# Two attentions on one core: first loads in halves, later weight rounding, and a third memory query moved into the attention turns

## The chip, the cores and the metric

The kernel runs on one core of a Trainium2 chip. The metric is device time in microseconds (us), the median of several executions. Profiles are of one execution; their times count from the start of the profiled span.

## The reference

Two independent attentions over 2048 tokens, 576 features, 32 heads of 18 features, all in float32. Their outputs stand side by side.

```
A:  q = x wq (32 heads);  k, v = x wk, x wv (one head for all)
    out = softmax(q k / sqrt(18)) v  wo
B:  q, k, v = x wq, x wk, x wv (32 heads each); 4 segments of 512 tokens; M = z = 0
    for s in 0..3:
        a_dot = causal softmax(q_s k_s / sqrt(18)) v_s
        a_mem = (phi(q_s) M) / (phi(q_s) z + 1e-6)        phi(t) = t + 1 if t > 0 else exp(t)
        o_s   = g a_mem + (1 - g) a_dot                   g = sigmoid(beta), one per head
        M, z += phi(k_s)^T v_s, sum of phi(k_s)
    out = o wo
```

Segment 0 has an empty memory. The memory queries of segments 1, 2 and 3 are the products `phi(q_s) M` (called num below) and `phi(q_s) z` (den).

## The kernel before, in words

**Stage 1, projections (0 to about 277 us of the span).** TensorE projects A's four chunks of 512 tokens (c = 0..3), then B's four segments (s = 0..3). A projection of 126 features is 14 matmuls, because operands are split in two rounded parts, high and low (`proj`, L261). For that, every input and weight is rounded by a copy (ScalarE or VectorE) and the rest is taken by a subtraction (VectorE or GpSimd).

- *First loads.* For c = 0 five pieces (k = 0..4, 128 rows each, the last 64) of A's weights `a_w` and of `a_xT` are loaded before anything can be multiplied. The weights and inputs go out on the SP queue, but the first input piece on ScalarE's queue.
- *B's weights* come in 15 pieces (`WPARTS`), loaded on GpSimd's queue (`load_wpart`) and rounded by `split_wpart`: a ScalarE copy (L251) and a GpSimd subtraction (L252). Pieces 10 to 14 are the query weights of the heads 0 to 27. They are rounded in segment 0, one behind each of the five key projections t = 0..4, and pieces 12 to 14 are loaded behind the first three. `pin` keeps an engine's pinned instructions in the order of the code, so a pinned copy that waits for its load holds up the pinned work behind it. Seven small loads of `gt` on GpSimd's queue follow.
- *A segment* is: five key projections (the fifth holds four query heads too), value projections of the first half of the heads, `last_key` and `fifth_bound` (small), second half of the values, four query projections. Every query projection is evacuated from PSUM (`pj`, four banks) by Relu, Abs, Exp and a rounding copy on ScalarE and three operations on VectorE.
- *The last segment* (s = 3) is written out on its own, pinned on TensorE. Between its query projections it asks the memory: `ask` multiplies phi(q) by M (one float32 matmul of 512 columns into `mm`, L444), `answer` scales the result on ScalarE (`nm`) and stores it; `total` multiplies by z (L592). `bound` (L588) multiplies magnitudes for the upper bound of the scores and needs the Abs of all five pieces. Only then come the first scores. The second half of the last segment's values is left to the attention stage (`late_value`, spread over its first 19 turns by `LATER`).

**Stage 2, attention (about 277 to 1350 us).** PE, ScalarE and VectorE follow an order written out by hand, in 416 turns of up to three score tiles. A block is four heads of a chunk of A (11 turns) or of a segment of B (2 turns). A0's turns are 0 to 10; B's blocks take turns 11 to 18, 30 to 37, 49 to 52, 64 to 71, 83 to 86 and so on. Per turn TensorE does the scores (L945 for A, L953 for B) into `E` (three tiles of two PSUM banks), at most one side job into the one bank `F`, and the products of the turn before the last into `O` (L993). ScalarE takes the exponentials (L963); one of three tiles is copied to SBUF by VectorE first (`W`, L960). In A-blocks two or three half tiles have their exponential computed on VectorE instead (`BY_DVE`, L919 to L926).

- *Side jobs.* From turn `ASK` = 20 on, `ask_memory` does the memory queries of the segments in `LATE_ASK` = (1, 2). Each segment has 6 steps of two halves; a turn takes a half: 4 column groups of 32 x 256 columns in float32 (L852). After the second half VectorE takes `F` out (L857, L861). Before the change a turn with B-scores takes no such half, so 24 halves occupy turns 20-29, 38-48 and 53-55. The queries' phi(q) come from DRAM (`qfB`, loaded by `load_qf` into a buffer `xh`, of which there are two, shared with the heads to be projected, `parts`).
- Then `out_proj` units fill the turns (L796, 8 instructions each, one unit per turn; 6 x 60 units), as soon as all five pieces of a chunk's heads are weighed by GpSimd (L780). What must happen at which turn is kept in a list `later`; `due` takes up to two entries a turn, and entries with a cost (the weighing) only when none of the next three turns is a B-turn and VectorE has no exponential open.

**The end.** Left-over units, then the output projections of A's last two chunks (L1280).

```
elif k >= ASK and all(its[n][0] == "A" for n, pr in turns[k]) and next(memory, None) is None:
    memory = None
```

## Time and profile before

| | before |
| --- | --- |
| median of 3 runs | 1394.51 us (1393.42 to 1395.25) |
| the profiled execution | 1394.57 us; its span 1392.9 us |
| granted TensorE clock | 0.999 |
| busy: TensorE / ScalarE / VectorE / GpSimd | 99% / 87% / 74% / 19% of the span |
| first matmul of a projection | 6.43 us |
| first scores (turn 0) | 276.80 us |
| first out_proj unit (turn 64) | 444.28 us |
| start of the last turn (415) | 1349.93 us |

A line of the timeline or of the chain begins with start and duration in us, then engine, line of the kernel, operation, what is written <- what is read. In brackets stands the idle time before it and what ended it. In the table of windows each engine has its busy us and, in brackets, its number of instructions.

### The profile page before, as it was taken

What the parts mean: (1) busy time and instruction counts of PE and PEld (TensorE: products, weight loads), DVE (VectorE), ACT (ScalarE), POOL (GpSimd) and SP (SyncE); (2) the same over time, 40 slices, a digit from 0 to 9 for tenths busy, and PEclk for the clock granted to TensorE, in tenths of its full rate; (3) what the DMA queues carried; (4) which work ended last, traced back from release to release, by engine and by line L of the source; (5) the groups of instructions that cost most, each with busy time, mean ns of one, the idle gap of its engine ahead of it and who ended that gap; (6) DMA issues with size and microseconds to landing.
All of it is one profiled execution on the core that took longest, in us unless ns stands there. A gap on an engine that the chain in (4) does not pass through costs nothing.

```text
span 1392.9 us, 41210 instructions
## 1 busy us (share of the span) xinstructions
PE 1379.1 (99%) x17455; PEld 835.6 (60%) x17455; DVE 1032.6 (74%) x1509; ACT 1205.8 (87%) x1497; POOL 260.5 (19%) x388
## 2 busy tenths in 40 slices
PE   9999999999999999999999999999999999999998
PEld 6778888755554555555555555555555555555558
DVE  6565463388787887777888877876878778887884
ACT  4543453599999999999999999999999999999992
POOL 2462120012313211312110022113010220001002
PEclk9999999999999999999999999999999999999999
DMA  9876556575564545332322442232103321120023
GB/s 285 261 230 185 180 198 204 188 208 181 153 182 158 147 145 162 101 113 77 105 67 71 141 152 63 85 120 79 52 35 100 104 76 42 31 71 21 18 64 132
DMA packets 88638, 173.67 MB, mean 125 GB/s; under 512 B 12308, under 2 KB 20109, under 8 KB 88018
## 3 DMA queue, kind: packets, MB, share of 16 engines
q1 hardware_dynamic: 81614, 158.91, 36.6%
q0 software_dynamic: 2368, 7.13, 1.8%
q10 hardware_dynamic: 4464, 4.92, 1.1%
q8 instruction: 139, 2.28, 0.7%
q14 instruction: 53, 0.43, 0.1%
HBM read 99.65 MB, written 70.67 MB: 122 GB/s over the span
## 4 chain that ended last, share of the span: by engine, by line
PE 88%; DVE 4%; ACT 3%; DMA 2%; issue 1%; POOL 1%; SPq 0%; DVEq 0%; POOLq 0%; ACTq 0%
PE O L993 33%; PE E L945 20%; PE F L796 11%; PE pj L261 11%; PE E L953 3%; ACT P L963 3%; PE nd L513 2%; DVE W L960 2%; PE pj L513 2%; PE E L1280 2%; PE pj L293 1%; PE F L852 1%; PE F L513 1%; DMA wr<-b_w 1%; DMA vseg<-vB 0%
## 5 line engine op out<-in xcount | busy, mean ns | idle before, releaser
L963 ACT ACTIVATE P<-E 128x1024 f32<-128x1024 f32 (+1 forms) x800 | 783.4, 1066 | 2.0 <-PE E L945 1.6
L960 DVE COPY W<-E 128x1024 f32<-128x1024 f32 (+2 forms) x416 | 453.1, 1089 | 142.2 <-PE E L945 84.1
L993 PE MATMUL O<-P,VA 128*32 128x256 f32 x7504 | 506.8, 379 | 0.0
L963 ACT ACTIVATE P<-W 128x1024 f32<-128x1024 f32 (+1 forms) x330 | 366.8, 1112 | 6.8 <-DVE W L960 6.3
L993 PEld LDWEIGHTS O<-P,VA 128*32 128x32 f32 x7504 | 258.8, 110 | 137.7 <-issue 4.7
L945 PE MATMUL E<-xl,kstA 56*128 56x512 f32 x1920 | 317.3, 430 | 2.1 <-ACT P L963 1.8
L945 PEld LDWEIGHTS E<-xl,kstA 56*128 56x128 f32 x1920 | 155.0, 184 | 159.1 <-issue 94.7
L968 POOL TENSOR_SCALAR_AFFINE_SELECT P<-P 128x256 f32<-128x256 f32 (+1 forms) x192 | 94.6, 493 | 393.4 <-ACT P L963 384.1
L780 POOL TENSOR_TENSOR xh<-xh,rb 126x512 f32<-126x512 f32 (+1 forms) x55 | 70.7, 1308 | 428.7 <-DVE PD L926 185.1
L796 PE MATMUL F<-woB,xh 126*32 126x192 f32 (+1 forms) x1920 | 126.6, 338 | 0.0
L993 PE MATMUL O<-PD,VA 128*32 128x256 f32 x688 | 88.9, 379 | 0.0
L796 PEld LDWEIGHTS F<-woB,xh 126*32 126x32 f32 (+1 forms) x1920 | 38.6, 108 | 74.8 <-issue 69.6
L993 PE MATMUL O<-P,vseg 128*32 128x256 f32 (+2 forms) x1536 | 81.4, 344 | 0.3
L127 DVE TENSOR_TENSOR qp<-pj,qp 126x512 fp32r<-126x512 f32 (+1 forms) x54 | 36.9, 686 | 54.4 <-ACT ph_e L408 32.8
L1002 DVE COPY oe<-O 128x512 f32<-128x512 f32 x64 | 44.2, 691 | 42.6 <-PE O L993 40.8
L261 PE MATMUL pj<-xh,wBh 128*126 128x512 f32 x180 | 72.5, 403 | 0.0
L919 DVE TENSOR_SCALAR PD<-E 128x512 uint32<-128x512 f32 x86 | 59.2, 688 | 16.5 <-PE E L945 14.9
L261 PE MATMUL pj<-xh,wBl 128*126 128x512 f32 x180 | 71.0, 394 | 0.0
L125 ACT CAST qp<-pj 126x512 fp32r<-126x512 f32 (+1 forms) x54 | 31.5, 584 | 42.6 <-PE pj L261 32.6
L993 PEld LDWEIGHTS O<-P,vseg 128*32 128x32 f32 x1536 | 49.1, 110 | 25.3 <-issue 1.8
L796 PE MATMUL F<-woA,xh 126*32 126x192 f32 (+1 forms) x960 | 63.9, 338 | 0.0
L924 DVE SCALAR_TENSOR_TENSOR PD<-PD,n 128x512 f32<-128x512 f32 x86 | 59.5, 692 | 3.0
(238 smaller groups left out, 1570.1 us busy)
## 6 DMA issues: line engine op xcount, KB each, us to landing
stB<-kB SPq DMA_DIRECT2D x96, 144.0 KB
stB<-qB SPq DMA_DIRECT2D x32, 288.0 KB
xl<-qA SPq DMA_DIRECT2D x30, 288.0 KB
oA<-oe SPq DMA_DIRECT2D x32, 256.0 KB
oB<-oe SPq DMA_DIRECT2D x32, 256.0 KB
qA<-qp SPq DMA_DIRECT2D x16, 504.0 KB
kB<-qp SPq DMA_DIRECT2D x16, 504.0 KB
qB<-qp SPq DMA_DIRECT2D x16, 504.0 KB
```

What stands on the lines that cost most here:

```text
L261: hold(nc.tensor.matmul(dst, w[:, c0 : c0 + M], x, start=i == 0, stop=i == len(ops) - 1))
L513: nc.tensor.matmul(pj[:, :n], x, w, start=m == 0, stop=m == len(ops) - 1)
L780: ins = tc.keep_in_program_order(nc.gpsimd.tensor_tensor(dst, a, b, op=op))
L796: nc.tensor.matmul(dst[32 * j : 32 * j + 32], parts[ab, c][: RT[t], t, r0 : r0 + 32], wo[ab][: RT[t], t, c0 : c0 + n], start=start, stop=stop,
L919: v.tensor_scalar(y, e, EXP_A, EXP_B, op0=ALU.mult, op1=ALU.add)
L924: lambda: stt(p, p, POLY[1], u, op0=ALU.add, op1=ALU.mult),
L945: nc.tensor.matmul(e[:, j], kstA[rows, 128 * kt : 128 * kt + 128], st[rows, h, :], start=True, stop=True)
L960: gate.append(nc.vector.tensor_copy(src[:, hs, :n], e[:, hs, :n]))
L963: nc.scalar.activation(p[:, hs, :n], src[:, hs, :n], AF.Exp, scale=SCALE)
L968: nc.gpsimd.affine_select(diag, diag, pattern=[[0, 2], [0, m], [1, 128]], base=0, channel_multiplier=-1, compare_op=ALU.is_ge, fill=0.0)
L993: nc.tensor.matmul(o[32 * j : 32 * j + 32, q0 : q0 + n], v, p[:, j % 2, p0 : p0 + n], start=m == hf == 0, stop=last and hf == 1,)
L1002: nc.vector.tensor_copy(osb, o)
```

## The change

- *First loads:* the first piece (k = 0) of inputs and weights is loaded in two halves of 64 rows, one half on SP's queue, one on ScalarE's, the inputs first. The other pieces stay on SP's queue.
- *B's query weights:* pieces 10 and 11 are rounded behind the key projections t = 1 and t = 3 of segment 0, pieces 12, 13 and 14 ahead of the value projections i = 1, 2, 3. The loads of 12 and 13 follow 10 and 11, the load of 14 follows 12.
- *Last segment:* `ask`, `answer`, `total` and the den store are gone. Its phi(q) are stored to `qfB[3]`, and `LATE_ASK` becomes (1, 2, 3). The condition that a turn be all A is dropped, so 36 halves occupy turns 20 to 55 without a gap. `load_qf(3)` comes at turn 32 or later, once segment 1 is answered. `place` (when a chunk's heads may be loaded into a buffer `xh`) now waits for the answers of segment 2 for the first chunk and of segment 3 for the second.
- *Turn 0:* a tile of `E` is allocated and left unused, so that the first scores go to the second and third tile; the late value work stands ahead of the third score tile; no tile is copied by VectorE; and the first half tile of block (A, 0, 0) is no longer given to VectorE's exponential.

```diff
-LATE_ASK, ASK = (1, 2), 20
+LATE_ASK, ASK = (1, 2, 3), 20
@@ first loads
-                for k in range(5):
+                for rows, queue in ((slice(0, 64), nc.sync), (slice(64, 128), nc.scalar)):
+                    queue.dma_start(xraw(0, 0)[rows], a_xT[rows, :C])
+                    queue.dma_start(raw[0][rows, 0, :CA], a_w[rows, :CA])
+                for k in range(1, 5):
                     load_part(raw[0][:, k, :CA], a_w, 0, CA, k, nc.sync)
-                    load_part(xraw(0, k), a_xT, 0, C, k, nc.sync if k else nc.scalar)
+                    load_part(xraw(0, k), a_xT, 0, C, k, nc.sync)
@@ key projections of segment 0
-                if s == 0:
-                    split_wpart(10 + t)
-                    if t < 3:
-                        load_wpart(12 + t)
-            if s and not last:
+                if s == 0 and t in (1, 3):
+                    split_wpart(10 + t // 2)
+                    load_wpart(12 + t // 2)
+            if s:
                 nc.sync.dma_start(qfB[s][: RT[4], 4], fs[4][: RT[4]])
@@ value projections
             for i in range(1, 4):
+                if s == 0:
+                    split_wpart(11 + i)
+                    if i == 1:
+                        load_wpart(14)
                 values(i, 0)
@@ query projections of the last segment
-                answer = ask(t - 1 if t else 4, pin)
                 if t < 2:
                     (fifth_bound if t else last_key)(pin)
-                if t == 3:
-                    pu, pd = (ps.tile([128, C], F32, name="nd", bufs=2) for _ in range(2))
-                    for i in (0, 1, 2, 4):
-                        total(pd, i)
                 e = negative(pj[:126], 126, pin)
                 magnitude(t, pj, pin)
-                fs[t] = phi(pj[:126], 126, "qf", 5, pin, e)
-                answer()
+                qp = split2(pt, pj[:126], 126, pin)
+                store_parts(qp, 0, 126, qB[s], 7 * t, 7)
+                f = phi(pj[:126], 126, "qf", 5, pin, e)
+                nc.sync.dma_start(qfB[s][:126, t], f[:126])
                 if t == 3:
+                    _, pu = (ps.tile([128, C], F32, name="nd", bufs=2) for _ in range(2))
                     for i in range(5):
                         bound(pu, i, pin)
-                    answer = ask(3, pin)
-                    total(pd, 3)
                     pin(nc.vector.tensor_reduce(fm[:, 1 + s : 2 + s], pu, axis=AX.X, op=ALU.max))
...
@@ attention
-        return [x for n, x in enumerate(BY_DVE) if n < 2 or (c, hg) in third]
+        return [x for n, x in enumerate(BY_DVE) if (n or c or hg) and (n < 2 or (c, hg) in third)]
...
-            return (ab, c) in parts or len(parts) - filled[0] // FILL < 2 and asked[0] >= min(2, len(parts) + 1)
+            return (ab, c) in parts or len(parts) - filled[0] // FILL < 2 and asked[0] >= min(3, len(parts) + 2)
...
         at(ASK + 4, 0, lambda: True, lambda k: load_qf(2))
+        at(ASK + 12, 0, lambda: asked[0] >= 1, lambda k: load_qf(3))
...
+            if k == 0:
+                psE.tile([128, 2, 512], F32, name="E")
+            exps = []
+            for i, (n, pr) in enumerate(turns[k]) if k < len(turns) else []:
+                if k == 0 and i == 2:
+                    late_values(k)
+                exps.append(scores(its[n], pr, i == 1 and k > 0))
...
-            elif k >= ASK and all(its[n][0] == "A" for n, pr in turns[k]) and next(memory, None) is None:
+            elif k >= ASK and next(memory, None) is None:
                 memory = None
```

More of the change, by code (lines that the diff above doesn't have):

```diff
@@ L438, in magnitude @@
                 hold(nc.scalar.activation(aqs[t][:R], pj[:R], AF.Abs))
-            def ask(t, hold=lambda ins: ins):
-                R = RT[t]
-                pn = ps.tile([128, C], F32, name="mm", bufs=1)
-                hold(
-                    nc.tensor.matmul(
-                        pn[:R], Mst[:R, t].rearrange("p h d -> p (h d)")[:, :R], fs[t][:R], start=True, stop=True
-                    )
-                )
-                def answer():
-                    nm = p2.tile([128, C], F32, name="nm", bufs=2)
-                    hold(nc.scalar.activation(nm[:R], pn[:R], AF.Copy, scale=gt[:R, t : t + 1]))
-                    nc.sync.dma_start(numB[s][126 * t : 126 * t + R], nm[:R])
-                return answer
             for t in range(5):
@@ L588, in bound @@
                 hold(nc.tensor.matmul(pu[rows], kbB[:R, t], aqs[t][:R], start=t < 4, stop=t > 0))
-            def total(pd, t):
-                R, rows = RT[t], slice(32 * (t % 4), 32 * (t % 4) + 32)
-                pin(nc.tensor.matmul(pd[rows], zst[:R, t], fs[t][:R], start=t < 4, stop=t > 0))
             for t in range(4) if last else []:
@@ L626, in attention_pair_kernel @@
             if last:
-                nc.vector.tensor_scalar(dn, pd, 1e-6, None, op0=ALU.add)
-                nc.sync.dma_start(denB[s], dn)
                 def late_value(i, m0, m1, pj, v, xh=xh, xl=xl, value_sums=value_sums):
@@ L1206, in halve_heads, with late_values @@
             mixed(x[:88, 1], hi[:88, 1], raws[key], some[:88, 1:2])
-        for k in range(len(turns) + 2):
-            now[0] = k
-            exps = [scores(its[n], pr, i == 1) for i, (n, pr) in enumerate(turns[k])] if k < len(turns) else []
-            for i in (0, 2, 1) if len(exps) == 3 else range(len(exps)):
-                exps[i]()
-            if k in FLAG:
-                loose_flag(k)
+        def late_values(k):
             if k < len(LATER) and LATER[k]:
@@ L1220, in attention_pair_kernel @@
                 late_value(i, m0, m0 + m, pj, (pa.tile([128, D], F32, name="osb", bufs=2) if i > 1 else pa.tile([128, C], F32, name="oe", bufs=4))[:, :304] if m0 + m == 14 else None)
+        for k in range(len(turns) + 2):
+            now[0] = k
+            if k == 0:
[5 more added lines that the diff above has]
+                exps.append(scores(its[n], pr, i == 1 and k > 0))
+            for i in (0, 2, 1) if len(exps) == 3 and k else range(len(exps)):
+                exps[i]()
+            if k in FLAG:
+                loose_flag(k)
+            if k:
+                late_values(k)
             if k > len(turns):
```

5 lines of the change are left out of this document (removed).

## The prediction

> **What bounds the kernel now.** I read the page's shares first, then TensorE's waits in stage 1, then the chain around each edited place, then windows cut at turn boundaries.
>
> ```profile
> PE   9999999999999999999999999999999999999998
> ACT  4543453599999999999999999999999999999992
> PE O L993 33%; PE E L945 20%; PE F L796 11%; PE pj L261 11%; PE E L953 3%; ACT P L963 3%; PE nd L513 2%; DVE W L960 2%; PE pj L513 2%; PE E L1280 2%; PE pj L293 1%; PE F L852 1%; PE F L513 1%; DMA wr<-b_w 1%; DMA vseg<-vB 0%
> ```
>
> TensorE is busy in every slice and carries most of the chain that ended last; ScalarE joins it at 9 when the attention begins. So in stage 1 only TensorE time, or TensorE waiting, is worth anything. What it waited for up to turn 0:
>
> ```profile
> PE tr L432 <- DVE qf L416: 1.6, 1, 1.6
> PE pj L293 <- DVE wAh L230: 1.3, 1, 1.3
> PE nd L176 <- DVE gt L492: 1.1, 1, 1.1
> PE mm L444 <- DVE qf L416: 0.5, 1, 0.5
> ```
>
> The change touches the first, second and fourth of these. In the attention a turn costs what its kind costs, so I price it by windows: eight A-turns with a memory half, eight A-turns with an out_proj unit, eight bare B-turns (30-37), eight B-turns with a unit (64-71), then the four B-turns 49-52 (bare) and 83-86 (with a unit):
>
> ```profile
> 330.98:353.06 22.08, 22.08 (x308) 11.27 (x304) 21.18 (x33) 21.83 (x26) 0.00 (x0) 1.00 0.57 177
> 467.38:488.60 21.22, 21.22 (x309) 11.38 (x306) 19.17 (x28) 21.22 (x25) 0.00 (x0) 1.00 0.49 137
> 355.59:373.73 18.14, 17.61 (x254) 10.27 (x250) 10.98 (x12) 18.14 (x24) 10.19 (x22) 1.00 0.50 154
> 442.99:462.51 19.52, 19.33 (x316) 12.05 (x312) 11.06 (x12) 19.52 (x26) 10.55 (x22) 1.00 0.37 106
> 404.11:413.82 9.71, 9.11 (x125) 5.10 (x121) 5.89 (x8) 9.13 (x12) 4.28 (x10) 1.00 0.58 173
> 491.01:500.48 9.47, 9.47 (x157) 5.86 (x153) 5.31 (x6) 9.47 (x13) 4.64 (x10) 1.00 0.20 67
> ```
>
> First number: the length; then the engines' busy time. A-turns fill both TensorE and ScalarE. Bare B-turns fill ScalarE (18.14 of 18.14) and leave TensorE at most a little (17.61): a side job there is nearly, not quite, free.
>
> **The change part by part.**
>
> *First loads: -0.3 us.*
>
> ```profile
> 7.04 0.68 DVE L219 TENSOR_TENSOR xl<-wBl,xh 128x512 fp32r<-128x512 f32 x1
> 6.43 1.16 PE L293 MATMUL pj<-xh,wAh 128*114 128x512 f32 x4 [1.26 <-DVE wAh L230]
> 7.43 0.40 PE L293 MATMUL mm<-xh,wAh 128*126 128x512 f32 x1
> 7.78 0.49 PE L293 MATMUL pj<-xl,wAh 128*114 128x512 f32 x1
> ```
>
> The weights start TensorE (6.43); then it waits for VectorE's low part of the inputs, which ends at 7.72: the sixth matmul follows the fifth (7.43) after 0.35 us. Most of that, 0.3, is to be had if the inputs land well ahead of the weights and VectorE does `xl` first. The weights themselves are the same bytes on the same rings behind the inputs, so I leave 6.43 as it is. Ends: -0.6 (weights a half-load earlier) to +0.5 (one more issue ahead of them and of all later pieces). [...]
>
> *B's query weights: -1.6 us.*
>
> ```profile
> 87.45 7.32 DMA wr<-b_w
> 94.79 0.61 ACT L251 CAST wBh<-wr 128x504 fp32r<-128x504 f32 x1 [2.63 <-DMA wr<-b_w]
> 99.12 0.41 PE L432 MATMUL tr<-ident,qf 126*128 126x126 f32 x2 [1.61 <-DVE qf L416]
> ```
>
> The load of piece 13 takes 7.32 us, ScalarE's pinned rounding copy waits 2.63 us for it, the fifth key projection's evacuation stands behind that copy, phi(q) comes late, and TensorE's transposition waits 1.61. With pieces 12 to 14 rounded behind that evacuation the wait goes. The copies (0.61 each) and GpSimd subtractions are the same number, merely later; ScalarE has idle time there. What is late next is piece 14, a rival below. Ends: -1.6 and what that rival costs.
>
> *The last segment: -6.7 us.* The chain from the fourth query projection to the first scores, and ScalarE's work behind that projection:
>
> ```profile
> 268.47 3.25 PE pj L261 x14
> 271.71 0.86 PE mm L444 x2
> ...
> 274.41 0.43 PE nd L588 x2
> 274.84 1.05 PE mm L444 x2
> 275.90 0.98 PE nd L592 x2
> 276.87 0.42 PE E L945
> 271.75 0.60 ACT L408 ACTIVATE ph_e<-pj 126x512 f32<-126x512 f32 x1 [1.16 <-PE pj L261]
> 272.24 0.59 ACT L438 ACTIVATE aq<-pj 126x512 bf16<-126x512 f32 x1
> ```
>
> Between the projections three asks (0.86 each) and the 0.5 us wait of L444 go: 3 x 0.86 + 0.5 = 3.1; the small key work in those slots stays. Behind the last projection 5.15 us (271.72 to 276.87) stand before the scores. Of these two asks, the totals and their waits go: what must remain is Relu and Abs of the fourth piece (until 272.83, 1.1 us behind the projection) and two bounds (0.43), some 1.55 in all with a hand-over between engines. That makes 3.6 and, with the 3.1, 6.7. The first score tiles then don't wait for the fourth piece's Exp and phi, because the third tile's banks are used last, and late values stand ahead of it. Ends: -4.3 (only the asks' 5 x 0.86; the evacuation chain shows behind) and -7.1 (3.1 and all of the 5.15 but ScalarE's 1.1). SP's queue gets five `qfB` stores for five numerator stores and one den store less: no gain, no cost.
>
> *Twelve halves in B-turns: +2.4 us.*
>
> ```profile
> 378.99 0.96 PE L945 MATMUL E<-xl,kstA 56*128 56x512 f32 x6
> 380.14 0.64 PE L852 MATMUL F<-xh,woA 126*32 126x256 f32 x8 [0.19 <-DVE rb L861]
> 380.77 1.50 PE L993 MATMUL O<-P,VA 128*32 128x256 f32 x24
> 382.21 0.50 PE L945 MATMUL E<-xl,kstA 56*128 56x512 f32 x2
> ```
>
> A half costs 22.08/8 = 2.76 per A-turn against 21.22/8 = 2.65 for a unit: 0.11 more than a unit. B-turns 30-37 with units would take 19.52, with halves 19.52 + 8 x 0.11 = 20.4, against 18.14 now: +2.2. Turns 49-52: 9.47 + 0.43 - 9.71 = +0.2. Ends: 0 (all in ScalarE's shadow) and +5.8: a half is 8 instructions of the products' shape, and 24 of those took 382.21 - 380.77 = 1.44, so it is 0.48 on TensorE, twelve times, with nothing hidden. The 24 halves in A-turns stay in the same A-turns, and the last half stays in turn 55.
>
> *The planner.* The third query may delay out_proj only through buffers and due times. Chunk (B, 0) may be loaded when segment 2 is answered (half 24 in turn 43, stored at 45); its sums are inverted at 45 (finish 37, begin 39, +5, two parts), so its loads come at turn 46 either way. The weighing then runs where it ran, and units start in the same turn 64:
>
> ```profile
> 433.54 6.26 POOL L780 TENSOR_TENSOR xh<-xh,rb 126x512 f32<-126x512 f32 x5 [17.71 <-DVE PD L926]
> 444.28 0.53 PE L796 MATMUL F<-woB,xh 126*32 126x192 f32 x8
> ```
>
> GpSimd waited for VectorE (the last exponential of the block), not for a load, so SP being busier by `load_qf(3)` at turn 34 (126 partitions x 5 x 512 floats at most, 1.3 MB) is covered as long as the loads of `rb` land before 433. 0 us, with +2 if this is missed.
>
> *Turn 0: +0.2 us.* ScalarE gets one half tile back from VectorE (25 exponentials in the 21.22 us of the second window are 0.85 us each, so 0.4 for a half) in a block that starts with ScalarE waiting for scores; half of it shows. Ends 0 and +0.4.
>
> **Sum.** -0.3 - 1.6 - 6.7 + 2.4 + 0.2 = -6.0 us. The profiled execution took 1394.57 (span 1392.9; median of the runs 1394.51, the same): **1388.6 us**. Everything behind stage 1 is relative, turn after turn, so a gain ahead of turn 0 arrives at the end.
>
> **Rivals.**
>
> *Piece 14 lands too late (up to 1395.5).* Work of ScalarE and GpSimd around that place:
>
> ```profile
> 104.47 0.18 ACT L522 COPY kn<-nd 128x18 f32<-128x18 f32 x1
> ...
> 109.80 0.21 ACT L581 ACTIVATE gt<-gt 128x7 f32<-128x7 f32 x1 [4.55 <-DMA gt<-b_beta]
> 100.19 4.38 POOL L495 DMA_DIRECT2D gt<-b_beta  x7
> ```
>
> On GpSimd's queue its load now stands behind seven `gt` issues (4.38) and piece 12's subtraction, which waits for ScalarE: issued near 102, landed up to 7.3 us later, 109.4. If ScalarE takes that copy ahead of the value block's last evacuation, the key transposition that TensorE has near 103 waits for it: up to 6.9 us with the copy's own 0.61, 1388.6 + 6.9 = 1395.5. For: the copy stands ahead of that evacuation in the code. Against: ScalarE already stood 4.55 us for a load just here, behind that evacuation, and TensorE lost nothing.
>
> *Slower: memory halves starve B-turns (1397.6).* F is one bank; a half that follows two VectorE evacuations waits for them, and the turn stretches: the one from 378.99 to 382.21 above took 3.22 us against 18.14/8 = 2.27 bare. If all twelve do so: 12 x 0.95 = 11.4 instead of 2.4, -8.4 + 11.4 = +3.0, 1397.6. It decides the sign from 8.4/12 = 0.70 us per B-turn. Against: this happens once in six steps, and VectorE is busy only 10.98 of 18.14 us in B-turns.
>
> *The tail of stage 1 gains only its asks (1391.0):* -4.3 instead of -6.7, the evacuation of the fourth piece taking the place of the asks as what is last. Against: Abs stands second on ScalarE.
>
> *The planner misses turn 61 (1390.6):* the weighing may not run from turn 62 to 69, fewer units run in ScalarE's shadow and some ten more are left to the end: ten x (21.22/8 - 18.14/8)/2, 2 us.
>
> **How the numbers follow.** Forecast, with its own ends 1385.3 (-0.6 - 1.6 - 7.1 + 0) and 1391 (halves at 4.8): 0.63. Piece 14: 0.13, half of it beyond 1392. Starved B-turns: 0.10. Short tail: 0.09. Planner: 0.05. A difference under 0.2%, 2.8 us, can't be told from none. Below 1391.7 lie the forecast, the short tail, the planner and little of the others: faster 0.76; same 0.15, slower 0.09 from the two dear rivals. The range 1385.0 to 1394.0 leaves out the upper ends of these two and what lies below the forecast's lower end.
>
> **What would show it.** First scores near 268 us (276.87 - 0.3 - 1.6 - 6.7 = 268.3); no wait of L432 near 97; no ScalarE wait over 2 us ahead of the fifth key evacuation; the first `xl` matmul right behind the fifth; turns 30-37 in 20 to 20.5 us; first unit in turn 64; the last turn near 1344. Wrong: a TensorE wait for `kn` near 103, waits of L852 on VectorE in B-turns, B-stack waits at turns 11 or 15, since they come 9 us sooner.

## The result: slower, and the profile after

The changed kernel takes 1406.25 us (median of five runs, 1404.33 to 1411.34) against 1394.51 (also of five): a ratio of 1.0092, 95% interval 1.0075 to 1.0108. The forecast of 1388.6 was wrong in sign. The profiled execution took 1405.52, its span is 1403.8 us against 1392.9: 10.9 to explain. The page's row of TensorE in 40 slices and the shares of its chain:

```profile
PE   9998999999989999999999999999999999999998
...
PE O L968 33%; PE E L920 20%; PE F L771 11%; PE pj L261 11%; PE E L928 4%; ACT P L938 2%; PE pj L498 2%; PE nd L498 2%; PE E L1267 2%; DVE W L935 1%; PE F L827 1%; PE pj L296 1%; DMA sm<-oB 1%; PE F L498 1%; DMA xr<-a_xT 1%
```

Two slices of TensorE (the fourth and the twelfth, near 110 and 406 us) are at 8 where only the last was, and `DMA sm<-oB` and `DMA xr<-a_xT` have come into the chain. (Every line number behind the edits has moved: L945 is now L920, L993 L968, L852 L827, L522 L507, L537 L526, L432 L435, L513 L498.) The starts of the same work in both traces say where the 10.9 lie, and what the prediction had given for it:

| stretch | before | after | difference | predicted |
| --- | --- | --- | --- | --- |
| start to the last matmul of segment 0's fifth key projection | 93.2 | 95.7 | +2.5 | -0.3 |
| from there to segment 0's first query projection | 19.3 | 24.3 | +5.0 | -1.6 |
| from there to the first scores (turn 0) | 164.3 | 157.5 | -6.75 | -6.7 |
| turns 0 to 4 | 14.4 | 18.4 | +3.95 | +0.2 |
| turns 5 to 45 | 104.8 | 106.0 | +1.24 | +2.2 |
| turn 46 | 2.76 | 8.25 | +5.49 | 0 |
| turn 47 to the end | 994.1 | 993.6 | -0.5 | +0.2 |

The third row came as forecast; the fifth cost about half of what was forecast. Three others (the second, the fourth and turn 46) hold 14.4 us of loss and the first 2.5. TensorE's waits of the changed kernel, first up to turn 0, then in the attention (us in total, times, longest):

```profile
PE tr L526 <- ACT kn L507: 3.6, 2, 2.8
PE pj L261 <- DVE xh L213: 1.6, 1, 1.6
...
PE nd L577 <- ACT aq L441: 0.8, 1, 0.8
...
```

```profile
PE E L920 <- DVE W L935: 3.8, 1, 3.8
...
PE F L498 <- DVE sht L136: 1.6, 1, 1.6
```

The wait of L432 for `qf` (1.6) is gone, as meant; `kn`, the fourth slice's `xh`, `aq`, `sht` and `W` stand in its place. All of its waits together, without the 1.1 us of its first instruction, are 14.5 us where they were 6.5. The half clock costs up to 6.8 more, an estimate from the windows. Windows around them (length; busy us of TensorE, its weight loads, VectorE, ScalarE, GpSimd, each with the number of instructions; granted clock; DMA share; GB/s):

```profile
104.80:109.20 4.40, 1.07 (x8) 0.55 (x6) 0.54 (x3) 1.36 (x5) 0.56 (x2) 1.00 0.42 118
109.20:116.00 6.80, 6.55 (x27) 6.25 (x28) 2.58 (x6) 1.70 (x6) 1.17 (x1) 0.50 0.27 73
...
277.10:279.80 2.70, 1.45 (x6) 0.57 (x5) 2.22 (x4) 2.37 (x4) 0.00 (x0) 1.00 0.69 214
279.80:283.30 3.50, 3.09 (x13) 3.12 (x14) 1.38 (x3) 0.55 (x1) 0.00 (x0) 0.51 0.85 278
403.00:406.40 3.40, 0.00 (x0) 0.00 (x0) 1.64 (x3) 0.00 (x0) 0.00 (x0) 0.96 0.89 258
406.40:409.50 3.10, 3.05 (x26) 1.46 (x30) 3.06 (x7) 2.88 (x3) 0.00 (x0) 0.50 0.91 300
360.30:380.02 19.72, 19.72 (x317) 11.92 (x313) 14.20 (x17) 19.37 (x25) 10.75 (x23) 1.00 0.52 168
415.46:425.51 10.05, 10.05 (x157) 5.82 (x153) 6.65 (x9) 10.01 (x13) 4.82 (x11) 1.00 0.57 188
```

Behind three of the four places where TensorE stood (not behind the one near 61 us), the granted clock is 0.5: from 109.2 to 116.0, 279.8 to 283.3 and 406.1 to 409.5. TensorE is busy in nearly all of these stretches, and slower: the pairs of matmuls that fill F in turn 0 follow each other every 0.72 us here and every 0.40 in f_bank1, and first_only has 9 matmuls in the 3.40 us from 62.7 (clock 0.50) and 18 in the next 3.40 (1.00). By the latter, 13.65 us at half clock lose up to 6.8, an estimate. In the profile before the clock was 1.0 from 3.8 to 1389.6. The last two lines answer to the B-turns of the prediction: 19.72 where bare turns took 18.14, and 10.05 where they took 9.71.

The four places in the chain that ended last. Near 61 us, in part A:

```profile
52.84 0.34 SPq L131
...
53.23 7.75 DMA xr<-a_xT
...
61.01 0.44 DVE xh L213
...
62.22 1.86 PE pj L261 x7
```

A load of the input's fourth slice goes out only when SP has sent a store of queries, and lands 7.75 us later; VectorE's rounding of it is what TensorE waits for. In the kernel before, SP sent the last of these loads at 50.11, one store sooner:

```profile
50.11 0.38 SPq L200 DMA_DIRECT2D xr<-a_xT  x1
```

Near 109 us, in segment 0 (two answers, the chain and ScalarE's timeline):

```profile
96.91 3.59 POOL gt L480 x6
...
101.28 1.31 POOL wBl L252
...
102.87 0.56 POOL wr L242
103.43 4.90 DMA wr<-b_w
...
108.42 0.09 ACT wBh L251
...
109.45 0.38 PE tr L526
```

```profile
107.28 0.21 ACT L570 ACTIVATE gt<-gt 128x7 f32<-128x7 f32 x1 [4.85 <-DMA wr<-b_w]
...
107.67 0.18 ACT L507 COPY kn<-nd 128x18 f32<-128x18 f32 x1
...
108.42 0.61 ACT L251 CAST wBh<-wr 128x504 fp32r<-128x504 f32 x1 [0.56 <-DMA wr<-b_w]
```

The seven `gt` loads hold GpSimd's queue, the load of piece 14 (in two parts) goes out behind them and a subtraction at 102.87 and 103.43, the later part lands at 108.33, and the last `kn` stands behind its rounding. Ahead of that the planner put gt's exponent (L570), which waited 4.85 us, in front of the third `kn`. (The view names a weight load for that wait; the last of gt's own loads landed at 107.10, just ahead of it.) Turn 0:

```profile
277.12 0.39 PE L577 MATMUL nd<-aq,kbB 126*32 126x512 bf16 x2 [0.85 <-ACT aq L441]
277.55 1.06 PE L920 MATMUL E<-st,kstA 56*128 56x512 f32 x4
280.21 0.58 PE L498 MATMUL F<-woB,xh 128*128 128x288 f32 x1 [1.60 <-DVE sht L136]
...
285.22 0.50 PE L920 MATMUL E<-st,kstA 56*128 56x512 f32 x2 [0.65 <-ACT P L938]
```

After two score tiles the late value work wants F and waits 1.60 us for VectorE's `sht`. The last line is turn 1's third score tile, which waits for an exponential of ScalarE. Turn 46:

```profile
395.50 9.23 DMA sm<-oB
...
404.76 0.04 DVE sm L720
...
405.23 1.17 DVE W L935
...
406.45 0.80 PE E L920 x2
```

The denominators of B's first chunk are read (`sm`) only at 395.50; VectorE's reciprocal, in its fixed place in the order, waits for them, and the copy that frees a score bank stands behind it. Of SP's own rows, two of the changed kernel, one of its waits there, and the read of `sm` in the kernel before:

```profile
373.92 0.31 SPq L804 DMA_DIRECT2D xh<-qfB  x1
...
381.75 3.36 SPq L682 DMA_DIRECT2D stB<-kB  x3
```

```profile
SPq L682 <- DMA xh<-qfB: 4.9, 2, 4.7
```

```profile
381.96 0.89 SPq L731 DMA_DIRECT2D sm<-oB  x1
```

The load of segment 3's phi(q) (`xh<-qfB`) is sent at 373.92; SP waits 4.7 us for it before the keys of B's stack, whose queries stand between, go out at 381.75, and the read of `sm` follows 13.7 us behind those. It goes out 6.4 us ahead of the start of turn 46 (401.93), where it was 14.0 us ahead before (381.96 and 395.99).

### The profile page after: what moved, and what is told of

It reads as the page before. It is cut to its first block, busy times and chain, and to the rows that moved or that the text cites. A ratio compares the mean times of both kernels' runs of the same rounds, so it can differ in the third digit from the quotient of the medians.

```text
span 1403.8 us, 41367 instructions
## 1 busy us (share of the span) xinstructions
PE 1382.4 (98%) x17531; PEld 840.6 (60%) x17531; DVE 1032.8 (74%) x1507; ACT 1204.1 (86%) x1492; POOL 260.0 (19%) x389
## 4 chain that ended last, share of the span: by engine, by line
PE 89%; DVE 3%; DMA 3%; ACT 3%; issue 1%; POOL 1%; SPq 0%; DVEq 0%; ACTq 0%
PE O L968 33%; PE E L920 20%; PE F L771 11%; PE pj L261 11%; PE E L928 4%; ACT P L938 2%; PE pj L498 2%; PE nd L498 2%; PE E L1267 2%; DVE W L935 1%; PE F L827 1%; PE pj L296 1%; DMA sm<-oB 1%; PE F L498 1%; DMA xr<-a_xT 1%
## 5 line engine op out<-in xcount | busy, mean ns | idle before, releaser
L968 PE MATMUL O<-P,VA 128*32 128x256 f32 x7512 | 507.2, 379 | 0.0
L968 PEld LDWEIGHTS O<-P,VA 128*32 128x32 f32 x7512 | 259.6, 110 | 137.3 <-issue 5.1
L920 PE MATMUL E<-xl,kstA 56*128 56x512 f32 x1920 | 317.4, 430 | 5.8 <-DVE W L935 3.8
L920 PEld LDWEIGHTS E<-xl,kstA 56*128 56x128 f32 x1920 | 155.2, 184 | 162.4 <-issue 96.1
L968 PE MATMUL O<-PD,VA 128*32 128x256 f32 x680 | 87.9, 379 | 0.0
L968 PE MATMUL O<-P,vseg 128*32 128x256 f32 (+2 forms) x1536 | 81.2, 344 | 0.1
L894 DVE TENSOR_SCALAR PD<-E 128x512 uint32<-128x512 f32 x85 | 58.5, 688 | 18.4 <-PE E L920 16.5
L968 PEld LDWEIGHTS O<-P,vseg 128*32 128x32 f32 x1536 | 49.4, 110 | 25.6 <-issue 1.1
L938 ACT ACTIVATE PD<-W 128x512 f32<-128x512 f32 x85 | 60.1, 707 | 1.4 <-DVE W L935 1.4
```

The lines of the kernel that those rows point to most:

```text
L894: v.tensor_scalar(y, e, EXP_A, EXP_B, op0=ALU.mult, op1=ALU.add)
L920: nc.tensor.matmul(e[:, j], kstA[rows, 128 * kt : 128 * kt + 128], st[rows, h, :], start=True, stop=True)
L938: nc.scalar.activation(p[:, hs, :n], src[:, hs, :n], AF.Exp, scale=SCALE)
L968: nc.tensor.matmul(o[32 * j : 32 * j + 32, q0 : q0 + n], v, p[:, j % 2, p0 : p0 + n], start=m == hf == 0, stop=last and hf == 1,)
```

## Experiments

All ran five rounds against the kernel before, but for the last two, which ran once. Medians, us:

| kernel | median | before, same chip | ratio (95%) |
| --- | --- | --- | --- |
| first_only | 1398.30 | 1394.02 | 1.0033 (1.0021 to 1.0044) |
| round_only | 1398.31 | 1394.02 | 1.0036 (1.0023 to 1.0049) |
| attn_only | 1397.24 | 1394.02 | 1.0039 (1.0024 to 1.0053) |
| pu_other | 1406.59 | 1394.02 | 1.0092 (1.0078 to 1.0107) |
| f_bank1 | 1405.32 | 1394.49 | 1.0064 (1.0047 to 1.0082) |
| gt_behind | 1402.94 | 1394.49 | 1.0060 (1.0046 to 1.0074) |
| values_twice | 1406.91 | 1394.49 | 1.0091 (1.0078 to 1.0104) |
| inv_later | 1404.21 | 1394.49 | 1.0071 (1.0055 to 1.0087) |
| four_mended | 1390.39 | 1394.47 | 0.9976 (0.9966 to 0.9986) |
| xr_late | 1397.25 | 1394.47 | 1.0011 (1.0000 to 1.0021) |
| qf3_later | 1406.33 | 1394.47 | 1.0084 (1.0068 to 1.0099) |
| gt_exp_late | 1406.93 | 1394.47 | 1.0086 (1.0073 to 1.0099) |
| early_table, w_halves (one execution each) | 1396.36, 1394.59 | 1396.63 | |

### Each part alone

*first_only*: the kernel before with

```diff
-  for k in range(5): ... load_part(xraw(0, k), ..., nc.sync if k else nc.scalar)
+  for rows, queue in ((slice(0, 64), nc.sync), (slice(64, 128), nc.scalar)):
+      queue.dma_start(xraw(0, 0)[rows], ...); queue.dma_start(raw[0][rows, 0, :CA], ...)
```

> The kernel before with the halves of the first loads alone. Theory (each loss belongs to the part in whose stretch it lies): the SP queue gets its order from a planner, and with the halves one of the loads of a_xT's third slice stands behind three later stores, as in the changed kernel; the first matmul comes 0.2 to 0.3 us later (6.68 instead of 6.43) and TensorE waits 1.6 + 0.2 us near 61 us on VectorE's xh and xl of that slice. By it 1394.5 + 0.25 + 2.4 = 1397.2 (1396.5 to 1398). Rival one: the wait at 61 is not from the halves but from traffic of the other parts; then 1394.5 (1394.0 to 1395.0) and no gap near 61. Rival two, the prediction's: 1394.2.

*round_only*: the kernel before with

```diff
-  if s == 0: split_wpart(10 + t); ... load_wpart(12 + t)
+  if s == 0 and t in (1, 3): split_wpart(10 + t // 2); load_wpart(12 + t // 2)
...
   for i in range(1, 4):
+      if s == 0: split_wpart(11 + i); ... load_wpart(14)
       values(i, 0)
```

> The kernel before with the later rounding of B's query weights alone. Theory: 1.7 us are gained before 100 us, then TensorE waits 3.5 us in two pieces for kn on its transposition of the last keys, and its granted clock is 0.5 for about 7 us behind that, which costs another 3.4: 1394.5 - 1.7 + 6.7 = 1399.5 (1398 to 1401). Rival one: the wait is there but the half clock came from something else (the first loads' waits at 61, say): about 1396. Rival two, the prediction's sum: 1392.9, with no wait for kn.

*attn_only*: the changed kernel with these two edits taken back.

> The kernel before with the part of the last segment, turn 0 and the asks in the attention alone; loads and rounding as before. Theory: -6.75 in the last segment, +4.2 in turn 0 (waits and a granted clock of 0.5 for 3.5 us), +1.6 in turns 30 to 37, -0.5 at 40 and 41, +5.5 at turn 46: 1394.5 + 4.1 = 1398.6 (1397 to 1400). Rival one, the prediction's sum for this part: -6.7 + 2.4 + 0.2 = 1390.4. Rival two: the stall of turn 46 hangs on where the two earlier losses put the DMAs, and goes: 1393.1.

The three parts alone cost 4.28, 4.29 and 3.22 us: 11.8 together, and the whole change 11.7. Each part loses by itself. By these medians nearly nothing comes from their meeting; by the ratios the parts lose 15.0 us and the whole 12.8, so the meeting adds no loss either way. TensorE's waits in first_only up to turn 0:

```profile
PE pj L296 <- DVE wAh L230: 1.4, 1, 1.4
PE pj L261 <- DVE xh L213: 1.3, 1, 1.3
...
PE tr L435 <- DVE qf L419: 0.7, 1, 0.7
```

The wait of 1.3 us for `xh` is there with the halves alone, and behind it the clock was 0.5 from 62.7 to 66.1. In round_only TensorE waited 3.15 and 0.65 us for `kn`, and the clock was 0.5 from 107.5 to 110.9 (3.4 us for the 7 expected): the wait and the half clock of the theory, without anything of the other parts. In attn_only the first scores came 6.92 us sooner; turn 0 took back 3.49 of it, turn 1 0.79, and turn 46 4.58 (a wait of 2.69 and 3.4 us of half clock).

### The order of SP's queue, and the start

*xr_late*: the kernel before, first loads whole, but three loads of the fourth slice of `a_xT` kept behind the stores behind which the halves' plan has them:

```diff
+  behind_ = {1: (1, 1), 2: (2, 0), 3: (2, 1)}.get(k) if xT is a_xT else None
+  with tc.issue_after(stored[behind_].ins): load_part(xr, ...)
```

> The kernel before, with its first loads whole, but with the loads of the fourth slice of a_xT put into SP's queue where the halves' plan has them: each one place of the stores later. Theory: the cost of the halves lies in this order. TensorE waits 1.3 to 1.8 us at 61 us, as in first_only (1.29) and the changed kernel (1.56 + 0.23), and the clock may fall to 0.5 for one window there (1.7 more): 1394.5 + 1.3 to 3.5, so 1396.5 (1395.8 to 1398). Rival one: the halves' own traffic is the cause, and this order costs nothing: 1394.5. Rival two: the slices behind are late too, with a second wait near 42 or 63 as in one run: over 1398.

```profile
PE tr L434 <- DVE qf L418: 2.7, 1, 2.7
PE pj L262 <- DVE xh L214: 1.6, 1, 1.6
```

With the order alone TensorE waits 1.6 us for `xh` at 60.9, and 1.1 us more than before for `qf` at 102.75, with the clock at 1.0: turn 0 starts 3.6 us later in this trace. The median rises by 2.8, though the interval of the ratio begins at no difference; the wait itself is shown, what it costs over many runs is less sure than its size in one.

*w_halves* (one execution): the input whole on ScalarE's queue, only the weight piece in halves; SP's later order comes out as before.

```diff
+  nc.scalar.dma_start(xraw(0, 0), a_xT[:128, :C])
+  for rows, queue in (...): queue.dma_start(raw[0][rows, 0, :CA], a_w[rows, :CA])
```

> The kernel before with the first weight piece in halves on two queues and the first slice whole on ScalarE's queue; SP's order of a_xT's fourth slice comes out as in the kernel before. Theory (the order is the cost of the halves behind 23 us): no wait of TensorE near 61 and none longer than 1 us up to 93; the first projection of the second slice at 23.2 to 23.8, the last of the first stage at 93.0 to 93.8. Rival (any split of the first loads makes the later loads late): a wait of 1.3 us or more near 61. At the start the weights land at 5.4 to 5.9, so the first matmul comes between 6.0 and 6.5.

No wait near 61 us: TensorE's only waits over 0.3 us up to 130 are 1.07 and 1.35 at the start and 1.53 for `qf`. Turn 0 starts 0.30 later than before, all of it from the start. So, as far as one execution shows, the order is the cost behind 23 us, and splitting a load is not. At the start I had expected 6.0 to 6.5 and it was 6.80: a miss that the next run explains.

*early_table* (one execution): first_only with a tiny copy ahead, so that ScalarE's table is loaded early.

```diff
+  nc.scalar.copy(tiny, onest[:, 0:1])
```

> First_only with a copy of 32 values ahead of ScalarE's first cast, so that the load of its table no longer waits behind the first slice's DMA (4.58 to 4.85 us in the runs with halves, 1.24 in the kernel before). SP's order stays that of first_only. Theory one (the table load holds the first cast): the cast starts at 4.6 to 4.9 instead of 5.9 to 6.1, but the first matmul also needs the rounded weights, which VectorE starts at 6.05 to 6.6 with halves (5.80 before): first matmul 6.6 to 7.2, no sooner than 6.43 of the kernel before. Theory two (the table load alone is the loss): first matmul at 6.1 to 6.3.

ScalarE's first cast, VectorE's rounding of the weights and TensorE's first matmul, of early_table:

```profile
4.81 0.62 ACT L213 CAST xh<-wBl 128x512 fp32r<-128x512 f32 x1 [1.27 <-DMA wBl<-a_xT]
```

```profile
6.51 0.48 DVE L230 CAST wAh<-wBl 128x618 fp32r<-128x618 f32 x1 [5.43 <-DMA wBl<-a_w]
```

```profile
7.14 1.15 PE L298 MATMUL pj<-xh,wAh 128*114 128x512 f32 x4 [0.77 <-DVE wAh L230]
```

The cast comes 1.07 us sooner than in the changed kernel (5.88), and the first matmul does not: VectorE can start on the weights at 6.51, where it did at 5.80 before. In the changed kernel it is 6.05, in nine other runs with halves 6.17 to 6.61, in five without halves 5.48 to 5.80. The table load was a side show; in halves the first weight piece lands later, and the first matmul comes 0.25 to 0.8 us later than before. Why it lands later is not shown: the weights' second half is also issued later here, at 1.24 to 1.47 us where the whole piece went out at 0.82.

### Piece 14, gt and the clock

*gt_behind*: the changed kernel, with the block that loads `gt` moved behind the loop of values.

```diff
-  if s == 0: nc.vector.memset(gt, 0.0); for ...: pin(nc.gpsimd.dma_start(gt[...], ...))
   vch = ...; values(0, 0); ...; for i in range(1, 4): ...; values(i, 0)
+  if s == 0: nc.vector.memset(gt, 0.0); for ...: pin(nc.gpsimd.dma_start(gt[...], ...))
```

> The changed kernel with the seven small loads of gt behind the last rounding of B's query weights on POOL's queue, where they stood ahead of the load of piece 14. Theory: the piece's load goes out 3.6 us sooner (the seven took 3.59 us of POOL), its rounding on ScalarE and with it the last kn come about 3.5 us sooner, the waits of TensorE on its transpositions (2.75 + 0.83 us) shrink below 0.5, and the granted clock stays 1.0: 1406.25 - 3.3 - 3.4 = 1399.5 (1399 to 1401). Rival one: the piece's transfer (4.9 us) is slow because 16 engines are busy, and lands no more than 1 us sooner: 1405. Rival two: what TensorE waits for first is gt's exponent, which stands on ScalarE ahead of the third kn and waits for gt's own loads; it goes behind with them here, so this run cannot tell it from the theory.

One wait of 0.93 us is left, the clock stays 1.0 from 69.5 to 404.0, and the stretch from the fifth key projection to the first query projection takes 18.7 us for 24.3. So the `gt` loads and their exponent are the cause at this place, -5.6 there for the 6.7 expected, though not quite as the theory had it: counted from the fifth key projection, the piece's load goes out only 0.8 us sooner, not 3.6, and its later part lands 2.8 us sooner. The median fell by 3.3 only: in its trace the waits near 61 us cost more than in the changed kernel (0.84 and 2.23 us, with 6.8 us of half clock), and the fifth key projection's last matmul started at 100.9 for 95.7.

*gt_exp_late*: gt's exponent pinned to its place in segment 1; the loads stay.

```diff
-  nc.scalar.activation(gt, gt, AF.Exp, scale=-1.0)
+  pin(nc.scalar.activation(gt, gt, AF.Exp, scale=-1.0))
```

> The changed kernel with gt's exponent held in its place in segment 1; in the changed kernel the planner had put it ahead of the third kn on ScalarE, where it waited 4.85 us for gt's loads. The loads stay ahead of piece 14. Theory (piece 14 sets the end): TensorE no longer waits for the third kn, but as long in all for the fourth, behind the rounding of piece 14: one wait of 3.3 to 3.6 us that ends at the same time, and the half clock stays: 1406.2 (1405 to 1407). Rival (gt's exponent was the stall): the wait falls to the 0.8 us of the fourth and the clock stays 1.0: 1406.25 - 2.75 - 3.4 = 1400.1.

One wait of 4.20 us (3.3 to 3.6 expected) at the fourth transposition and 6.8 us of half clock; 1406.93. The exponent only covered the first part of the wait; piece 14 sets its end.

*values_twice*: the last value group of segment 0 summed twice over into the same bank.

```diff
-  value_sums(xh, xl, i, hf, pj)
+  [value_sums(xh, xl, i, hf, pj) for _ in range(2 if (s, i, hf) == (0, 3, 0) else 1)]
```

> The changed kernel with the 14 matmuls of the last value group of segment 0 issued twice over into the same bank (the second sum starts anew, so the values are the same); they stand ahead of the transpositions of kn and take 1.95 us. Piece 14 and kn come when they came. Theory: the half clock is the price of idle TensorE: its idle time there falls from 3.58 to about 1.6 us, the last transposition starts at the same time, and the granted clock stays 1.0 for the 6.8 us in which it was 0.5, so 28 matmuls more than before the change cost nothing and 3.4 us are gained: 1402.9 (1402.4 to 1404.6; the upper end if one of the two half windows stays). Rival: the clock does not hang on the idle time: 1406.2 to 1408.2.

(It issues 14 matmuls more than the changed kernel.) Windows of values_twice, ahead of and behind the wait:

```profile
107.80:112.00 4.20, 2.00 (x16) 1.44 (x15) 0.69 (x4) 1.73 (x7) 0.81 (x1) 1.00 0.26 90
112.00:119.30 7.30, 7.30 (x56) 7.12 (x55) 2.43 (x6) 2.13 (x6) 0.45 (x1) 1.00 0.44 129
```

The waits shrank to 1.54 and 0.66 us, and the clock stayed at 1.0 where it had been 0.5. The stretch up to the first query projection took 22.1 us for 24.3, with 1.95 us more work in it, so the half clock went with TensorE's idle time here, 3.6 us against 2.2, and not with the place. The other executions agree: the seven with 3.1 to 4.2 us of waits there (the changed kernel, round_only, pu_other, f_bank1, inv_later, qf3_later, gt_exp_late) all lost the clock; the other nine, with 0.3 to 2.7 there (some of it for `qf`, a few us earlier), did not. The time did not fall (1406.91): the saving of 2 us is within what the other three places vary from run to run, and in its trace the fifth key projection ended 1.5 later and TensorE stood another 1.34 us at 238 us.

### Turn 0

*pu_other*: the bound's sums taken from the other tile of the pair.

```diff
-  _, pu = (ps.tile([128, C], F32, name="nd", bufs=2) for _ in range(2))
+  pu, _ = (ps.tile([128, C], F32, name="nd", bufs=2) for _ in range(2))
```

> The changed kernel with the bound's sums of the last segment in the other bank of the pair nd, so that the late value work of turn 0 no longer writes into the bank that VectorE is still reading. The instructions and their order are the same on every engine. Theory: the wait of F for sht (1.60 us ahead of 280.21) goes, and with it the granted clock of 0.5 from 279.8 to 283.3, which cost 1.75: 1406.25 - 3.3 = 1402.9 (1402.2 to 1403.8). Rival one: the two waits of 0.85 and 0.65 that stay are enough for the clock: 1404.6. Rival two: the value work waits for something else, and nothing changes: 1406.2.

Nothing changed: F still waited 1.62 us for `sht`. The compiled addresses, of which the next expectation tells, show why: the unused tile takes no bank, and the sums sit in bank 0 either way. It serves as a second run of the changed kernel. So F was moved instead, *f_bank1*:

```diff
   if k == 0:
-      psE.tile([128, 2, 512], F32, name="E")
+      psE.tile([128, 2, 512], F32, name="E"), psO.tile([128, C], F32, name="O")
```

> The changed kernel with F, the tile that the late value work of turn 0 fills, in the other PSUM bank (the compiled addresses: the bound's sums in bank 0, F now in bank 1 where it was in bank 0; the swap of the pair nd had left the sums in bank 0). Every engine's instructions and order are the same. Theory: the wait of F for sht goes (1.60 us), and the half clock that began beside it (3.4 us long, 1.7 us lost): 1406.25 - 3.3 = 1402.9 (1402.2 to 1403.8). Rival one: the clock still falls, from the waits of 0.85 and 0.65 that stay: 1404.6. Rival two: the value work waits for something else: 1406.2.

The end of turn 0 in f_bank1:

```profile
279.78 0.40 PE L498 MATMUL F<-woB,xh 128*128 128x288 f32 x1
280.02 0.29 PE L498 MATMUL F<-woB,xl 128*128 128x288 f32 x1
```

F's matmuls follow the scores without a wait, and take 0.29 for 0.44: the clock is 1.0. Turn 0 is 0.44 us longer than before where it was 3.44 longer. Turn 1 stays 0.75 us longer (0.78): F's bank is not the reason for that. 0.65 us of it are the wait of its third score tile for ScalarE's exponential, which the changed kernel has too. The median of 1405.32 is only 0.9 below the changed kernel, for 3.3 expected; in its trace the half clock at turn 46 lasted 6.8 us instead of 3.4, and another 3.4 us came at 7.5, behind a wait of 1.95 at the start.

### Turn 46

*inv_later*: the reciprocals of B's first chunk three turns later.

```diff
-  d0, d1, d2, d3 = ... (2, 5, 3, 5) if (ab, c) == ("B", 0) else ...
+  d0, d1, d2, d3 = ... (2, 8, 3, 5) if (ab, c) == ("B", 0) else ...
```

> The changed kernel with the reciprocals of B's first chunk put on VectorE three turns later (turn 49 for 46); the loads and stores ahead of them keep their places in SP's queue. Theory: VectorE waited 3.85 us at turn 46 for the read of the denominators, which SP sent late behind the third memory half; three turns later it has landed, the wait and the half clock of 3.4 us go: 1406.25 - 3.8 - 1.7 = 1400.8 (1400 to 1402). Rival one: the wait moves to turn 49 (the read lands later still, behind other traffic): 1406. Rival two: the wait goes, but the outputs that follow come late and the first unit of the output projection slips from turn 64: 1403 to 1405.

The 5.49 us of turn 46 are gone (turn 47 starts 5.49 us sooner against turn 46's start than in the changed kernel), TensorE has no wait over 0.5 us from 280 to 470, and the clock stays 1.0 from 289.4 to the kernel's last microseconds. The median fell by 2.0, not 5.5: 2.3 came back in turns 0 and 1, where this execution's half clock lasted 10.2 us for 3.4.

*qf3_later*: the load of segment 3's phi(q) ten turns later, and the asks held for five.

```diff
-  at(ASK + 12, 0, lambda: asked[0] >= 1, lambda k: load_qf(3))
+  at(ASK + 22, 0, lambda: asked[0] >= 1, lambda k: load_qf(3))
-  elif k >= ASK and next(memory, None) is None:
+  elif k >= ASK and k not in range(44, 49) and next(memory, None) is None:
```

> The changed kernel with the load of the third memory half ten turns later (behind the reads of B's first denominators in SP's queue) and its asks five turns later (turns 49 to 60). Theory: the load is what made SP late at turns 36 to 43; without it the stores and reads go out some 8 us sooner, VectorE's reciprocals at turn 46 do not wait, nor does TensorE, and the clock stays: 1406.25 - 5.5 = 1400.8 (1400 to 1402.5). Rival one: SP is late from the four extra stores of the asks or the traffic of B's own stacks, and the wait of 2 to 4 us at turn 46 stays: 1405 to 1406.5. Rival two: the load now delays the asks themselves (TensorE waits for qf at turn 49): 1402 to 1404.

The wait at turn 46 is gone but for 0.4 us (turns 40 to 51 take 0.3 us less than before), and the read of `sm` goes out 10.8 us ahead of the turn, so the load was most of what made SP late there. But the time is the same, 1406.33, and for a reason that none of the three cases named: a wait later on. TensorE's waits near 460 us in qf3_later:

```profile
PE E L928 <- DMA stB<-kB: 3.3, 1, 3.3
...
```

and one of SP's from 400 to 462 us:

```profile
SPq L843 <- DMA denB<-rb: 4.1, 1, 4.1
```

A later stack of B lands late instead, with 6.8 us of half clock behind it: +6.2 between turns 60 and 80. Its loads stand behind an ask's store (L843), before which SP waited 4.1 us, until 444.80. The run also held the asks, and so this store, back by five turns; whether that or the moved load of 1.1 MB made the stack late was not tested. Moving the reader (inv_later) removes the wait at turn 46 without a new one.

### All four mended

*four_mended*: the changed kernel with the first loads whole, gt_behind, f_bank1 and inv_later.

> The changed kernel with all four losses mended: the first loads whole as before, gt's seven loads behind piece 14, F in the other bank, the reciprocals of B's first chunk three turns later. Theory (the parts add up, and nothing else is lost): against the kernel before, by stretches of the runs so far, -0.4 ahead of 93 us and -0.6 up to segment 1, -6.75 up to turn 0, +1.2 in turns 0 and 1, -0.3 at turn 4, +1.6 in turns 30 to 37, -0.5 and +0.3 behind them: 1394.5 - 5.4 = 1389.1 (1387.5 to 1391), no granted clock below 1.0 between 10 and 1380 us. Rival: a wait that stays at one of the four places still takes the clock down (each such window costs 1.7): 1391 to 1394.

```profile
PE tr L523 <- ACT kn L495: 1.2, 1, 1.2
```

1390.39 against 1394.47, 0.9976 (0.9966 to 0.9986): a little faster than the kernel before, and 15.9 us below the changed kernel. Taken singly, the three mends of gt, F and the reciprocals gained 3.3, 0.9 and 2.0 in the median, each less than its stretch, for in each of their profiles the other places together took more than in the changed kernel's; the profiled execution took 1389.12. The clock is 1.0 from 6.5 to 1385.5. The first scores come at 269.01 (276.80 before); turns 0 and 1 give 1.2 back and turns 20 to 60, with the halves, 1.6. TensorE still waits 1.2 us for `kn`, and the clock stays.

## Why the prediction was wrong, step by step

- *First loads, -0.3: failed.* The step read only the eight microseconds of the start. The first matmul, which it left at 6.43, comes at 6.68, since the weights land later in halves (VectorE starts on them at 6.05, before at 5.80); the 0.35 us between the fifth and the sixth matmul that it meant to close is 0.30 now (7.73 and 8.03), since VectorE still makes `xl` (7.29) behind the weights; and it did not look at what one more issue does to SP's planned order: its own end of +0.5, "one more issue ahead of them and of all later pieces", stopped there. Measured: +2.5 in the profile, +4.3 alone.
- *B's query weights, -1.6: the wait it named is gone, the rival came true.* The rival "Piece 14 lands too late" had place and mechanism right and a chance of 0.13. That the stretch missed the forecast by 6.6 us, close to the rival's cap of 6.9, is luck: about half of it is the clock, which the rival did not have. Its argument against, that ScalarE's wait of 4.55 for `gt` cost TensorE nothing, failed: that wait stood behind the last `kn` then, and moves ahead of the third when the roundings move. Measured: 3.6 us of waits and up to 3.4 of clock. The gain was also sized by one execution: with the old rounding the wait for `qf` was 1.61 us before, 0.88 in attn_only, 0.72 in first_only, 1.53 in w_halves, 2.73 in xr_late, and under 0.3 in early_table. With gt's loads out of the way (four_mended) the stretch takes 18.96 us for 19.31.
- *The last segment, -6.7: right*, -6.75 in the profile; -6.0 in the same stretch with this part alone (attn_only). Between the last projection's end (275.95) and the scores stand 1.6 us, where 1.55 was written.
- *Twelve halves in B-turns, +2.4: right*, a little high. 19.72 for eight turns where 20.4 was written, 10.05 for four against 9.9. L827's waits on VectorE, the sign of the rival "memory halves starve B-turns", are not there.
- *The planner, 0: bookkeeping right, cover wrong.* The first unit is in turn 64. But "SP being busier by `load_qf(3)` is covered as long as the loads of `rb` land before 433" asked for the wrong reader. The read of the denominators, with a fixed place for its consumer in VectorE's order, was the one without slack: 5.49 us.
- *Turn 0, +0.2: failed.* It counted ScalarE's half tile and not that the late value work, moved ahead of the third score tile, opens F while VectorE still reads the bound's sums in that bank: +4.2 in turns 0 and 1 together, of which 1.2 stay with F moved. What makes up these 1.2, beyond the 0.65 of waiting for ScalarE, was not tested.
- *Missing from the sum:* the clock. A wait of 1.29 us (first_only, near 61 us) was followed by 3.4 us at clock 0.5, which at half speed is up to 1.7 us lost, and the 13.65 us at 0.5 of the changed kernel's profiled execution by the same estimate up to 6.8. No step asked what a wait costs beyond its length.

## What to carry to other kernels

When a step is moved on an engine whose order is planned, compare the whole order of every queue before and after, not the moved step: here one more issue at the start put three later loads behind stores that they had stood ahead of, and moved roundings pulled a waiting exponent ahead of a needed copy. For a transfer added to a full queue, list the readers behind it by their slack; the one with a fixed slot on a busy engine is the one that stalls. And price a TensorE wait with the half clock that may follow it: here one of 1.29 us (first_only) was followed by 3.4 us at 0.5, up to 1.7 us by estimate, and one of 2.73 (xr_late) by none.

## What the hardware showed that I had not expected

The granted clock fell to 0.5 for 3.413 us (turn 0 and turn 46 of the changed kernel), 6.827 (near 109 us there) or 10.240 (inv_later), whole multiples of one length; in the changed kernel this stood behind waits of 0.85 and 1.60, of 3.8 and of 3.6 us. The length of a wait alone does not decide: 1.29 us near 61 us was followed by a fall in first_only and pu_other and by none in inv_later, values_twice and qf3_later, and 0.85 and 1.6 us in turn 0 were followed by a fall in seven executions and by none in gt_behind. The time stamps say more. In the trace of the changed kernel the clock falls at 109.172, 279.838, 406.132 and 1402.823 us: the later three lie 50.00, 87.00 and 379.00 times 3.4133 us behind the first. In that of the kernel before, its two changes, at 3.800 and 1389.611 us, lie 406.00 times that length apart. So I cut each execution into windows of that length, laid at its own changes. Turn 0 of the changed kernel, then of gt_behind, in these windows:

```profile
276.43:279.84 3.41, 1.45 (x6) 0.57 (x5) 2.26 (x4) 3.08 (x6) 0.00 (x0) 1.00 0.72 227
```

```profile
274.30:277.71 3.41, 2.53 (x14) 1.30 (x13) 1.45 (x3) 2.15 (x5) 0.00 (x0) 1.00 0.74 257
277.71:281.12 3.41, 1.79 (x13) 1.40 (x11) 3.02 (x6) 1.94 (x2) 0.00 (x0) 1.00 0.70 232
```

In the changed kernel both waits lie in one window, TensorE is idle for 1.96 of its 3.41 us, and the clock falls at its end. In gt_behind they lie in two windows, with 0.88 and 1.62 us idle, and it does not fall. Cut like this up to 1380 us, the traces of the kernel before and of the changed kernel have 803 windows at full clock. Behind three of them, with 1.96, 2.69 and 3.41 us of idle TensorE, the clock fell; behind the other 800, with at most 1.61, it did not. (The ends of matmuls are modelled, so the idle times are not exact.) In first_only a window with 1.63 us idle was followed by a fall, in gt_behind the one above with 1.62 by none. This is a count over the traces of these kernels; no limit, and no rule by which the clock is set, is shown by it. The same wait was followed by a fall in one execution and by none in another, and a fall costs by estimate up to 1.7 us for each 3.41 us at 0.5. This bears on values_twice too: its waits came to lie in two windows, with 1.12 and 1.07 us idle, and in one window they might have cost the clock.

The changed kernel, with four such places, ranges over 7.0 us in five runs where the kernel before ranged over 1.8; but in 23 later runs the kernel before ranged over 7.4 as well, so how much of the spread is the clock's is not shown.
